# A third inner seven-product in a tuned Strassen-like MLP: product 2 of mixer 1 over a base in SBUF, with VectorE's sums reordered

## The chip, the cores and the metric

The kernel runs on one core of one Trainium2 chip. The metric is the device time of one execution in microseconds (us). Executions of one kernel mostly agree within 0.3%. Unless said otherwise, times are medians of several executions; the traces come from one profiled execution each.

In the profiles PE is TensorE (matmuls), PEld its weight loads, DVE is VectorE (here sums and additions), ACT is ScalarE (here copies and Gelu), POOL is GpSimd, and SP issues transfers (DMA). SBUF and PSUM are the two memories on the chip in which the kernel's tiles lie; its matmuls all write to PSUM. A "gap" below is the time by which a matmul starts later than the usual spacing of the matmuls before it would let it.

## The reference

The program is a pre-norm block: linear attention with a residual, then a token-mixing MLP with a residual. Only the first matmul of the MLP (here "mixer 1") matters for this change.

```python
def _B_ref(x, w1, b1, w2, b2):          # x: 1 x 2048 x 1024, w1: 2048 x 3584
    h = _layernorm(x, axis=-1)
    u = jnp.einsum("bsd,sf->bdf", h, w1) + b1      # mixer 1
    u = _gelu(u)
    y = jnp.einsum("bdf,fs->bds", u, w2) + b2      # mixer 2
    return (lambda x, *d: x.transpose(*d))(y, 0, 2, 1)
```

## The kernel before

Each block product is done with seven matmul products in place of eight (the Winograd form of Strassen). Two neighbouring block products ("sts") make one round. Products 1 and 5 of both are taken together and split once more into seven inner products of half the width: an `Inner` set. While TensorE works on a set, 16 matmuls of another product ("fill") are put between its seven steps, in four portions.

An `Inner` set keeps its results in two PSUM tiles: `ae` holds quarters a and e, `bc` holds quarters b and c. Keep `bc` in mind: b and c are two halves of one 512-column fp32 tile, which the kernel counts as one PSUM bank (its constant `BANK` is 512).

```python
psy = ...tile_pool(name="psy", bufs=NT, space=PSUM, ...)   # C;  NT = 2
psx = ...                                                  # B
psw = ...                                                  # A
psz = ...                                                  # inner sets (tags z0, z1): 8 such tiles in all

class Inner:
    ...
    def i1(self):
        ae = psz.tile([P, BANK], F32, tag="z0", bufs=1, name="psI0")
        bc = psz.tile([P, BANK], F32, tag="z1", bufs=1, name="psI1")
        self.a, self.e, self.b, self.c = ae[:, 0:HW], ae[:, HW:CW], bc[:, 0:HW], bc[:, HW:CW]
        self.mm(1, self.a, True)
        nc.scalar.copy(self.b, self.a)
    def i6(self):
        self.mm(6, self.b, False)
        nc.scalar.copy(self.c, self.b)
    def i2(self):
        self.mm(2, self.a, False)
        self.sink(0, 0, self.a)
    def i5(self):
        self.mm(5, self.e, True)
        self.es = cpool.tile([P, HW], F32, tag="es", name="es")
        nc.scalar.copy(self.es[:], self.e)            # ScalarE: "es"
    def i7(self):
        self.mm(7, self.c, False)
        self.sink_sum(1, 1, self.c, self.es[:])       # VectorE reads c
    def i3(self):
        self.mm(3, self.b, False)                     # TensorE writes b
        self.sink_sum(0, 1, self.b, self.es[:])
    def i4(self):
        self.mm(4, self.c, False)
        self.sink(1, 0, self.c)

    # Quad: the order of one set with its fill portions 0..3
    for f in (n.i1, after1, 0, n.i6, n.i2, 1, n.i5, n.i7, flush, 2, n.i3, 3, n.i4, flush): ...

    # Quad.run, one round of mixer 1 (cut)
    interleave(self.in1, [st.p4 for st in pend], start)   # set of product 1, fill: product 4 of the round before
    ...
    interleave(self.in5, [st.p6 for st in self.sts])      # set of product 5, fill: product 6
    ...                                                   # here VectorE sums for the next round (pre)
    for st in self.sts: st.p2()                           # 16 matmuls of 512 columns into A (PSUM)
    ...
    for st in self.sts: st.p7(...)
    for st in self.sts: st.p3()                           # the last evacuation is left to the next round
```

## Time and profile before

| | before |
|---|---|
| time, median of 3 | 571.77 us |
| span in the trace | 570.7 us |
| TensorE busy | 562.1 us (98%) |
| six rounds of mixer 1 with inner products | 143.0 us in this trace |
| a steady round | 23.57 us |

The head of the profile page (engine, busy time, share of the span, number of instructions), and the chain of waits by engine (the chain that ended last):

```profile
PE 562.1 (98%) x3049; PEld 289.9 (51%) x3064; DVE 388.2 (68%) x734; ACT 274.1 (48%) x573; POOL 1.8 (0%) x8
...
PE 87%; DVE 5%; DMA 4%; ACT 2%; issue 1%; SPq 0%; DVEq 0%
```

TensorE is the limit: it is nearly always busy, and 87% of the chain is its own work. VectorE and ScalarE matter only where TensorE waits for them.

The six rounds, each a stretch from its first inner matmul to the next round's. The columns are the stretch, its length, and the busy time of each engine with the number of instructions:

```profile
core 0: us, PE busy (x) PEld busy (x) DVE busy (x) ACT busy (x) POOL busy (x), PEclk, DMA share, GB/s
255.71:279.29 23.58, 23.58 (x137) 13.28 (x136) 14.78 (x32) 9.95 (x22) 0.00 (x0) 1.00 0.29 90
279.29:303.19 23.90, 23.80 (x137) 13.29 (x136) 12.17 (x26) 10.76 (x24) 0.00 (x0) 1.00 0.28 88
303.19:328.00 24.81, 23.80 (x138) 13.29 (x136) 14.10 (x28) 12.15 (x27) 0.00 (x0) 1.00 0.27 85
328.00:351.57 23.57, 23.57 (x138) 13.27 (x136) 12.80 (x26) 11.62 (x25) 0.00 (x0) 1.00 0.29 90
351.57:375.14 23.57, 23.57 (x137) 13.30 (x136) 12.81 (x26) 11.10 (x25) 0.00 (x0) 1.00 0.28 90
375.14:398.71 23.57, 23.57 (x137) 13.29 (x136) 7.59 (x15) 11.54 (x25) 0.00 (x0) 1.00 0.31 80
sum 143.00, PE 141.89 PEld 79.74 DVE 74.26 ACT 67.12 POOL 0.00; mean PE 23.65 PEld 13.29 DVE 12.38 ACT 11.19 POOL 0.00
```

Three rounds take 23.57 us. Rounds 2 and 3 take longer; there VectorE's timeline shows 1.58 and 2.49 us of idle that ended with the landing of weights, and evacuations queued behind it.

The waits of TensorE, window of mixer 1 (who waited for whom: us in total, times, longest):

```profile
PE psI L209 <- ACT psI L242: 1.0, 1, 1.0
PE psA L209 <- ACT psB L318: 0.4, 1, 0.4
```

One set of product 1 in a steady round, from the timeline (start, duration, engine, instruction; in brackets the idle time before it and what ended it). The matmuls at 331.69 are the set's seventh product, those at 332.88 its third:

```profile
331.69 0.60 PE L209 MATMUL psI<-hi,is 128*128 128x256 f16 x4
331.89 0.37 ACT L255 COPY es<-psI 128x256 f32<-128x256 f32 x1
...
332.12 0.81 PE L209 MATMUL psC<-hT,wq 128*128 128x512 f16 x3
332.39 0.43 DVE L209 TENSOR_TENSOR psA<-psI,es 128x256 f32<-128x256 f32 x1 [3.24 <-PE psI L209]
...
332.88 0.60 PE L209 MATMUL psI<-hE,is 128*128 128x256 f16 x4
```

The three fill matmuls start at 332.12. In this kernel 512-column matmuls start 0.216 us apart (16 take 3.455 us in the chain), so the third product (`psI<-hE,is`) could start at 332.77; it starts at 332.88. The profile prints no idle before it, because a 512-column matmul is drawn 0.379 us long, 0.163 us longer than its spacing.

### The profile page before, as it was taken

How to read it: one execution, taken by the hardware profiler on the slowest of the kernel's cores; microseconds unless marked ns; L12 is line 12 of the kernel's file. 1: busy time of each engine (PE TensorE's matmuls, PEld its weight loads, DVE VectorE, ACT ScalarE, POOL GpSimd, SP SyncE). 2: the span in 40 equal slices, each digit the busy share in tenths (PEclk: the TensorE clock that was granted, in tenths of full speed). 3: DMA queues.
4: the chain of work that ended last, by engine and by line, in shares of the span. 5: the costliest groups of instructions: out<-in, count | busy, mean ns of one | idle time of the engine just before them, and what ended most of it. 6: DMA issues, size and time to landing. Idle time of an engine off the chain costs nothing.

```text
span 570.7 us, 8133 instructions
## 1 busy us (share of the span) xinstructions
PE 562.1 (98%) x3049; PEld 289.9 (51%) x3064; DVE 388.2 (68%) x734; ACT 274.1 (48%) x573; POOL 1.8 (0%) x8
## 2 busy tenths in 40 slices
PE   8999999999999999999999999999999999999997
PEld 3444444454444444456555565554445655645643
DVE  6898888544776798965654735633989749658725
ACT  5747777667776777545445354453220311311211
POOL 1000000000000000000000000000000000000000
PEclk9999999999999999999999999999999999999999
DMA  9833432025673841104041340413892932912111
GB/s 302 288 74 76 92 74 38 19 94 180 189 231 102 276 168 74 56 0 149 1 148 40 108 148 1 148 57 75 211 250 92 241 92 75 284 48 75 38 46 47
DMA packets 86087, 67.13 MB, mean 118 GB/s; under 512 B 15762, under 2 KB 80032, under 8 KB 86048
## 3 DMA queue, kind: packets, MB, share of 16 engines
q1 hardware_dynamic: 85312, 65.94, 39.8%
q10 hardware_dynamic: 672, 0.66, 0.3%
q8 instruction: 24, 0.39, 0.3%
q14 instruction: 15, 0.12, 0.1%
q0 software_dynamic: 64, 0.01, 0.0%
HBM read 54.54 MB, written 8.91 MB: 111 GB/s over the span
## 4 chain that ended last, share of the span: by engine, by line
PE 87%; DVE 5%; DMA 4%; ACT 2%; issue 1%; SPq 0%; DVEq 0%
PE acc_t L209 16%; PE psC L209 14%; PE psB L209 12%; PE psI L209 11%; PE psA L209 6%; PE psB L797 4%; PE psC L797 4%; PE psA L797 4%; DMA wq<-in_B_w_dram 3%; PE acc_t L721 2%; PE psB L299 2%; PE psA L299 2%; PE acc_t L1066 2%; PE psE L797 2%; PE psC L299 2%; PE kvps L750 1%
## 5 line engine op out<-in xcount | busy, mean ns | idle before, releaser
L209 PEld LDWEIGHTS <-wq 128*128 128x128 bf16 (+1 forms) x653 | 63.4, 98 | 55.6 <-issue 1.0
L209 PEld LDWEIGHTS <-sa 128*128 128x128 f16 x651 | 63.7, 98 | 54.7
L209 PE MATMUL acc_t<-wo_sb,pqT 128*128 128x512 f16 x256 | 55.6, 379 | 0.0
L209 PEld LDWEIGHTS <-is 128*128 128x128 f16 x376 | 36.7, 98 | 19.4 <-issue 4.6
L209 PE MATMUL psC<-gs,wq 128*128 128x512 f16 (+2 forms) x210 | 45.0, 365 | 0.0
L209 PE MATMUL acc_t<-xnT,wq_sb 128*128 128x512 bf16 x188 | 43.1, 379 | 0.2
L209 PEld LDWEIGHTS <-pqT 128*128 128x128 bf16 x256 | 25.0, 98 | 30.5 <-issue 0.6
L171 DVE TENSOR_SCALAR e_sb<-e_sb 128x512 bf16<-128x512 bf16 x64 | 18.6, 290 | 27.9 <-ACT e_sb L167 27.3
L167 ACT ACTIVATE e_sb<-acc_t 128x512 bf16<-128x512 f32 x40 | 23.9, 597 | 24.5 <-PE acc_t L209 12.0
L797 PEld LDWEIGHTS <-xs 128*128 128x128 f16 x208 | 20.1, 98 | 23.3 <-DVE xs L783 1.3
L209 DVE TENSOR_TENSOR ot<-ot,hr 128x512 bf16<-128x512 bf16 (+2 forms) x27 | 11.2, 414 | 28.1 <-ACT ot L431 27.7
L209 DVE TENSOR_TENSOR e<-psI,es 128x256 f32<-128x256 f32 x20 | 8.5, 424 | 31.9 <-ACT es L255 19.3
L209 PEld LDWEIGHTS <-wq_sb 128*128 128x128 bf16 x192 | 18.5, 98 | 23.0 <-issue 1.3
L333 ACT COPY psC<-psB 128x512 f32<-128x512 f32 x22 | 12.5, 570 | 35.3 <-PE psB L209 30.5
L209 PE MATMUL psB<-hT,sa 128*128 128x512 f16 x112 | 28.7, 379 | 0.0
L209 DVE BATCH_NORM_STATS2 hst<-acc_t 128x6 f32<-128x512 f32 x32 | 21.3, 692 | 8.7 <-ACT h_bf L209 8.6
L797 PE MATMUL psA<-wkv,xnT 128*128 128x512 bf16 x98 | 26.4, 379 | 0.3
L209 DVE TENSOR_TENSOR psA<-psI,es 128x256 f32<-128x256 f32 x18 | 7.8, 433 | 26.9 <-PE psI L209 21.8
L209 PE MATMUL psA<-hO,wq 128*128 128x512 f16 x112 | 25.3, 379 | 0.4 <-ACT psB L318 0.4
L242 ACT COPY psI<-psI 128x256 f32<-128x256 f32 x19 | 6.9, 361 | 38.8 <-PE psI L209 38.8
L209 PE MATMUL psB<-hO,sa 128*128 128x512 f16 x112 | 25.3, 379 | 0.0
L209 PE MATMUL psC<-hT,sa 128*128 128x512 f16 x112 | 25.3, 379 | 0.0
(184 smaller groups left out, 1009.3 us busy)
## 6 DMA issues: line engine op xcount, KB each, us to landing
wq<-in_B_w_dram SPq DMA_DIRECT2D x14, 1024.0 KB, 7.9
wq<-in_B_w_dram SPq DMA_DIRECT2D x8, 1792.0 KB, 9.4
xr<-in_A_x_dram SPq DMA_DIRECT2D x16, 256.0 KB, 5.1
rdb<-rd_dram SPq DMA_DIRECT2D x32, 128.0 KB, 3.8
h_dram<-h_bf SPq DMA_DIRECT2D x16, 256.0 KB, 2.0
hr<-h_dram SPq DMA_DIRECT2D x32, 128.0 KB, 2.5
out_dram<-ot SPq DMA_DIRECT2D x31, 128.0 KB, 1.7
x_sb<-in_A_x_dram SPq DMA_DIRECT2D x15, 256.0 KB, 3.0
```

The source lines that it names most:

```text
L167: pin(nc.scalar.activation(e_sb[:], src, ACT.Exp))
L171: pin(nc.vector.tensor_scalar(e_sb[:], e_sb[:], 1.0, PHI_EPS, ALU.min, ALU.add))
L209: return (lambda *a, **kw: pin(op(*a, **kw))) if self.always or Held.on else op
L242: nc.scalar.copy(self.b, self.a)
L299: pe.matmul(ps[:, cols], lhsT=lhs[:, k, :], rhs=mv(k)[:, cols], start=(start and k == 0), stop=(k == self.nk - 1), skip_group_check=True,)
L333: nc.scalar.copy(self.C[:], self.B[:])
L721: mm = nc.tensor.matmul(pp[:, 0:CW], lhsT=xnT[:, kt, i * P:(i + 1) * P], rhs=wkv[:, kt, c * CW:(c + 1) * CW], start=(kt == 0), stop=(kt == ...
L750: pin(nc.tensor.matmul(kv_ps[b][:, sl, :], lhsT=pks[i % NPK][:, j * P:(j + 1) * P], rhs=vaugs[i % NVA][:, j, :], start=False, stop=(i == N ...
L797: pin(nc.tensor.matmul(ps[:], lhsT=lhs[:, k, :], rhs=rhs[:, k, :], start=(start and k == 0), stop=(k == hk2 - 1), skip_group_check=True,))
L1066: nc.tensor.matmul(qp[:, 0:SW], lhsT=wq_sb[:, kt, j * P:(j + 1) * P], rhs=xnT[:, kt, u * SW:(u + 1) * SW], start=(kt == 0), stop=(kt == ND ...
```

## The change

Product 2 becomes a third inner set (`Inner2`). Its base, the 512-column result A of product 1, no longer lies in PSUM but in SBUF (tiles a0 and a1), and VectorE adds the set's four results to it, in six additions of 256 columns. The fill of this set is product 7. That replaces 16 matmuls of 512 columns by 28 of 256 columns, that is, by 14 of 512. VectorE's sums for the next round move behind the evacuations (the steps that take finished results out of PSUM), and the evacuation of the round's last shared tile goes behind six of those sums. At the head, the last two combinations come after the last normalization.

```diff
+    class Inner2(Inner):
+        def i5(self):
+            self.mm(5, self.e, True)
+            for m in range(2):
+                self.sink(m, 1, self.e)
+        def i7(self):
+            self.mm(7, self.c, False)
+            self.sink(1, 1, self.c)
+        def i3(self):
+            self.mm(3, self.b, False)
+            self.sink(0, 1, self.b)
...
-        def begin(self):
-            self.A = psw.tile([P, BANK], F32, tag="w", name="psA1")
+        def begin(self, based=False):
+            if based:
+                self.A = pools["t"].tile([P, BANK], F32, tag=f"a{self.p % 2}", name="a1")
+            else:
+                self.A = psw.tile([P, BANK], F32, tag="w", name="psA1")
...
+        def sink2(self, m, h, ps):
+            t = self.sts[m].A[:, self.cols(h)]
+            dve.tensor_tensor(t, ps, t, ALU.add)
+
+        def run1(self, pend, nxt, on_p4):
+            def starting():
+                self.asums(5)
+                self.in5 = Inner(sts, 5, self.mov5, "i5", self.sink5, self.sum5)
+                self.in5.sums()
+                pend[1].p3_evac()
+                for st in sts:
+                    st.begin(based=True)
+            self.interleave(
+                self.in1, [st.p4 for st in pend], {"in": starting, "mid": partial(sts[0].asum, 6)}
+            )
+            sts[1].asum(6)
+            self.asums(7)
+            in2 = Inner2(sts, 2, self.mov2, "i1", self.sink2, None)
+            in2.sums()
...
+            self.interleave(self.in5, [st.p6 for st in sts])
...
+            self.interleave(in2, [st.p7_fill for st in sts], {
+                "third": lambda: sts[0].evac(0, 0, sts[0].A), "out": lambda: sts[1].evac(0, 0, sts[1].A),
+            })
+            if nxt is not None:
+                nxt.begin1()                      # sums of the next round's set of product 1
+            sts[0].p3()
+            sts[1].p3_mm()
... (the old run, with p2, and the order of the head are left out)
```

More of the change, by code (lines that the diff above doesn't have):

```diff
@@ L349, in p2, with p7_fill @@
                 self.evac(0, 0, self.A)
+        def p7_fill(self, ks=None, late=None):
+            self.mm(7, self.C, False, ks)
+            if self.whole(ks):
+                self.parts = [(0, CW, self.C)]
+                late.append(partial(self.evac_shared, 1, self.C))
         def p7(self, cut=None):
@@ L444, with __init__ @@
     class Quad:
-        def __init__(self, sts, mov1, mov5):
+        def __init__(self, sts, mov1=None, mov5=None, mov2=None):
             self.sts = sts
-            self.mov1, self.mov5 = mov1, mov5
-            self.after1 = nop
+            self.mov1, self.mov5, self.mov2 = mov1, mov5, mov2
         def cols(self, h):
@@ L467, in sum5, with interleave @@
             dve.tensor_tensor(self.sts[m].e[:, self.cols(h)], ps, es, ALU.add)
-        def pre(self, m):
-            if m == 5 and self.mov1 is not None:
-                self.in1 = Inner(self.sts, 1, self.mov1, "i1", self.sink1, self.sum1)
-                self.in1.sums()
-            for st in self.sts:
-                st.asum(m)
-            if m == 5:
-                self.in5 = Inner(self.sts, 5, self.mov5, "i5", self.sink5, self.sum5)
-                self.in5.sums()
-        def interleave(self, n, fs, after1=nop):
+        def interleave(self, n, fs, at={}):
             steps = [(f, k) for f in fs for k in range(self.sts[0].nk)]
@@ L495, in flush @@
                     late.pop(0)()
-            for f in (n.i1, after1, 0, n.i6, n.i2, 1, n.i5, n.i7, flush, 2, n.i3, 3, n.i4, flush):
-                fill(f) if isinstance(f, int) else f()
-        def asums_once(self, m):
-            for st in self.sts:
-                if m not in st.lhs:
-                    st.asum(m)
+            for f in (
+                n.i1, "in", 0, n.i6, n.i2, 1, n.i5, n.i7, flush, 2, "mid", n.i3, "third", 3, n.i4, "out", flush,
+            ):
+                if isinstance(f, int):
+                    fill(f)
+                else:
+                    (at.get(f, nop) if isinstance(f, str) else f)()
         def asums(self, m):
@@ L561, in run_first @@
             self.interleave(self.in5, [st.p6 for st in sts])
-            nxt.in1 = Inner(nxt.sts, 1, nxt.mov1, "i1", nxt.sink1, nxt.sum1)
-            nxt.in1.sums()
-            nxt.asums(5)
+            nxt.begin1()
             for st in sts:
@@ L568, in run_first @@
             sts[1].p3_mm()
-            def after1():
-                sts[1].p3_evac()
-                nxt.in5 = Inner(nxt.sts, 5, nxt.mov5, "i5", nxt.sink5, nxt.sum5)
-                nxt.in5.sums()
-                nxt.asums(6)
-            nxt.after1 = after1
-            return sts, nxt
-        def run(self, pend, nxt, on_p4=nop, before_p7=nop, on_p7=nop, cut=None):
-            interleave = self.interleave
-            if self.mov1 is not None:
-                def start():
-                    self.after1()
-                    for st in self.sts:
-                        st.begin()
-                interleave(self.in1, [st.p4 for st in pend], start)
-                self.asums_once(7)
-            else:
-                for st in self.sts:
-                    st.p1()
-                for st in pend:
-                    st.p4()
+            return sts, nxt
@@ new lines, in begin1 @@
+        def begin1(self):
+            self.in1 = Inner(self.sts, 1, self.mov1, "i1", self.sink1, self.sum1)
+            self.in1.sums()
+        def sink2(self, m, h, ps):
+            t = self.sts[m].A[:, self.cols(h)]
+            dve.tensor_tensor(t, ps, t, ALU.add)
+        def run1(self, pend, nxt, on_p4):
+            sts = self.sts
+            def starting():
[12 more added lines that the diff above has]
+            in2.sums()
@@ L594, in run @@
             on_p4()
             nxt = nxt()
-            for st in self.sts:
+            for st in sts:
                 st.shared_tile()
-            interleave(self.in5, [st.p6 for st in self.sts])
-            self.sts[0].finish()
-            self.asums_once(3)
-            pre = nxt.pre if nxt is not None else (lambda m: None)
-            pre(5)
-            for st in self.sts:
-                st.p2()
-            pre(6)
-            before_p7()
-            for st in self.sts:
-                st.p7(cut if st is self.sts[-1] else None)
@@ L609, in run @@
-            on_p7()
-            last = self.sts[-1]
-            for st in self.sts:
-                if st is last and nxt is not None:
-                    st.p3_mm()
-                    nxt.after1 = st.p3_evac
-                else:
-                    st.p3()
-            return self.sts, nxt
+            self.interleave(self.in5, [st.p6 for st in sts])
+            sts[0].finish()
+            self.asums(3)
+            self.interleave(in2, [st.p7_fill for st in sts], {
+                "third": lambda: sts[0].evac(0, 0, sts[0].A), "out": lambda: sts[1].evac(0, 0, sts[1].A),
+            })
@@ L619, in moving @@
+            if nxt is not None:
+                nxt.begin1()
+            sts[0].p3()
+            sts[1].p3_mm()
+            return sts, nxt
     def moving(E, O, T2, T3, T4):
@@ L1280, in h_scale, with normalize_h, combine_h @@
                 hs.activation(sc_all[:, i:i + 1], lnv[:], ACT.Exp, scale=-0.5)
-            def normalize_h(i):
+            def normalize_h(i, combined=True):
                 dst = hE if i % 2 == 0 else hO
                 hv.tensor_scalar(dst[:, i // 2, :], h_bfs.pop(i)[:], mv_all[:, i, 0:1], sc_all[:, i:i + 1], ALU.subtract, ALU.mult)
-                if i % 2 == 1:
-                    q = i // 2
-                    combine(hE[:, q, :], hO[:, q, :], hT2[:, q, :], hT3[:, q, :], hT4[:, q, :], hv)
+                if i % 2 == 1 and combined:
+                    combine_h(i // 2)
+            def combine_h(q):
+                combine(hE[:, q, :], hO[:, q, :], hT2[:, q, :], hT3[:, q, :], hT4[:, q, :], hv)
             for c in range(NDC):
@@ L1294, in first_sums @@
             def first_sums():
-                cur = Quad([Mixer1(0), Mixer1(1)], None, None)
+                cur = Quad([Mixer1(0), Mixer1(1)])
                 for m in (5, 6, 7, 3):
@@ L1348 @@
                     h_scale(i - 1)
-                    normalize_h(i - 2)
+                    normalize_h(i - 2, False)
                     normalize_h(i - 1)
@@ L1358 @@
             h_scale(NS - 1)
-            normalize_h(NS - 1)
+            normalize_h(NS - 1, False)
+            combine_h(NSP - 2)
+            combine_h(NSP - 1)
     accx.close()
@@ L1378 @@
     mov5, sums5 = inner_moving(hE[:, :, CW:D], NSP, inner1, "hi5")
+    mov2, sums2 = inner_moving(hO[:, :, 0:CW], NSP, inner1, "hi2")
     NQ1 = NFP // 2
@@ L1390, in quad1 @@
     def quad1(u):
-        return Quad([Mixer1(2 * u), Mixer1(2 * u + 1)], mov1, mov5)
+        return Quad([Mixer1(2 * u), Mixer1(2 * u + 1)], mov1, mov5, mov2)
     Held.on = True
@@ L1396 @@
     pend, nxt = cur.run_first(quad1(1), sums1)
+    sums2()
     for u in range(1, NQ1):
         cur = nxt
-        pend, nxt = cur.run(pend, lambda: quad1(u + 1) if u + 1 < NQ1 else None, on_p4=next_load1(u + 1))
+        pend, nxt = cur.run1(pend, lambda: quad1(u + 1) if u + 1 < NQ1 else None, next_load1(u + 1))
     Held.on = False
+    pend[1].p3_evac()
     for st in pend:
```

## The prediction

> **What bounds the kernel now.** TensorE: the page gives it 98% of the 570.7 us span, and the chain of waits gives it 87%. In mixer 1 the timeline repeats one round per pair of products; six rounds use the inner products (255.7 to 398.7 us). By windows they take 23.58, 23.90, 24.81, 23.57, 23.57, 23.57 us (sum 143.0), TensorE busy throughout except about 1 us in the third. VectorE is busy about 12.8 us of a round, ScalarE about 11.2. So only matmul time, and waits that the change adds or removes, count.
>
> **Removed and added per round.** Out: product 2, 16 matmuls of 512 columns, 3.455 us in the chain. In: seven inner products of four 256-column matmuls, 0.433 us each, 3.03 us; plus one more of the 0.1 us gaps that the timeline shows before the last-but-one inner product of every such set. Net -0.32 us: an undisturbed round should take 23.25 us. VectorE gains four inner sums (0.34 us each, start to start) and six 256-column additions (0.42 us): about 3.9 us a round, to roughly 16.7 of 23.5, not a limit by throughput. ScalarE gains two 0.36 us copies. Once, VectorE also pays 2.8 us for the moving sums of product 2.
>
> **Removed waits.** In rounds 2 and 3 VectorE sat waiting for weights (1.58 and 2.49 us of idle ended by the DMA), with evacuations queued behind; that reached TensorE as 0.23 and 0.97 us before an inner sixth product. The sums now come after the evacuations, about 4 us after the landing: about 1.5 us saved. At the head, putting the last two combinations after the last normalization should remove the 0.39 us wait of product 2 for the copy psB.
>
> **New wait.** The instruction order puts the Gelu of the previous round's last shared tile before the copy "es" of inner product 1 (before, it came two copies earlier, right after the first), because VectorE now evacuates that tile only after six sums. From the trace's start-to-start times I work out: es at 4.5 us into the round instead of 3.9; VectorE's next addition at 4.9, then a 0.61 us product-6 sum put between the two additions, the second at 5.9 instead of 5.5; ScalarE's queue then delivers the first copy of the inner set of product 5 at about 7.95 to 8.05 instead of 7.64. Its sixth product starts 0.41 us after that copy starts (seen in rounds 2 and 3), so at about 8.4 instead of 8.12: a stall of 0.2 to 0.4 us per round, eating most of the 0.32. Round 1, with the 2.8 us of moving sums in front, loses about 0.5. The Trainium skill ("TensorE: Matmul & The Clock Gate", Engine queue depths) says ScalarE and VectorE are strict FIFO; the trace agrees: evacuations start only after the stalled sums (rounds 2 and 3).
>
> **Sum.** Rounds: 6 x 23.25 + 0.5 + 5 x 0.28 = 141.4, against 143.0: -1.6. Head -0.4. Mixer 2 unchanged. Predicted 569.8 us, 8 in 10 between 567.8 and 571.4. Chances: faster by over 2% 0.01, within 2% 0.98, slower 0.01.
>
> **What would show it.** Right: rounds of about 23.5 us; idle TensorE of 0.2 to 0.4 us before the second inner product of the set of product 5, released by the ScalarE copy psI; no VectorE idle ended by the weight DMA; no gap in product 2 of the first round. If that idle is absent, rounds are 23.25 and the time is about 568.
>
> **What would make it wrong.** ScalarE slower reading the base from SBUF than from PSUM, lengthening every copy in that queue; the sums after the third set meeting the shared-tile evacuations later than I place them; the head or the start of mixer 2 (its first matmuls now stand inside the last round) stalling on VectorE.

## More of the kernel before

The Trainium skill ("Perfetto Trace Analysis", Tensor Engine Instruction) says that the end of a TensorE instruction is estimated, not observed. The trace agrees: the drawn end of the third fill matmul (332.12 + 0.81 = 332.93) lies after the start of the next one. A wait of up to 0.16 us can hide in that.

## The result, and the profile after

| | before | after |
|---|---|---|
| time, median (4 runs each) | 571.61 us | 574.27 us |
| six rounds in the trace | 143.0 us | 145.53 us |
| a steady round | 23.57 us | 24.20 us |
| VectorE busy in a steady round | 12.8 us | 16.4 us |

The ratio is 1.0045 (95% interval 1.0028 to 1.0063). A ratio is the mean time of one kernel's fast runs over that of the other's in the same rounds, so it is not quite the ratio of the medians. The change made the kernel slower by 2.7 us, or 0.45%; that is outside the noise. 569.8 us had been predicted, with a range up to 571.4.

The same parts of the page after:

```profile
PE 561.0 (98%) x3136; PEld 296.6 (52%) x3136; DVE 412.2 (72%) x798; ACT 278.5 (49%) x585; POOL 1.8 (0%) x8
...
PE 89%; DVE 5%; ACT 2%; DMA 1%; issue 1%; SPq 0%; DVEq 0%; ACTq 0%
```

The rounds of the changed kernel (rounds 2, 4 and 5 left out, they are 24.21, 24.21 and 24.20):

```profile
core 0: us, PE busy (x) PEld busy (x) DVE busy (x) ACT busy (x) POOL busy (x), PEclk, DMA share, GB/s
255.35:279.86 24.51, 23.41 (x149) 14.46 (x148) 18.36 (x40) 11.34 (x26) 0.00 (x0) 1.00 0.28 87
...
304.07:328.27 24.20, 23.40 (x149) 14.47 (x148) 16.40 (x37) 11.91 (x27) 0.00 (x0) 1.00 0.27 88
...
376.68:400.88 24.20, 23.72 (x151) 14.62 (x150) 14.95 (x33) 12.51 (x27) 0.00 (x0) 1.00 0.30 77
sum 145.53, PE 140.72 PEld 86.90 DVE 98.94 ACT 71.50 POOL 0.00; mean PE 23.45 PEld 14.48 DVE 16.49 ACT 11.92 POOL 0.00
```

The matmul work did shrink, yet every round is longer. TensorE's waits in mixer 1:

```profile
PE psI L209 <- DVE a L209: 4.8, 11, 0.8
PE psI L209 <- DVE e L209: 0.5, 1, 0.5
```

TensorE now waits for VectorE's additions, eleven times in the six rounds (the single wait for `e` comes before them). In which place? The set of product 1 in round 3:

```profile
307.43 0.72 ACT L407 ACTIVATE gE<-t,b_sb 128x512 f16<-128x512 f32 x1
307.76 0.60 PE L209 MATMUL psI<-hi,is 128*128 128x256 f16 x4
308.05 0.67 ACT L407 ACTIVATE gO<-psC,b_sb 128x512 f16<-128x512 f32 x1
...
308.19 0.81 PE L209 MATMUL psC<-hT,wq 128*128 128x512 f16 x3
308.62 0.36 ACT L255 COPY es<-psI 128x256 f32<-128x256 f32 x1
...
309.01 0.43 DVE L209 TENSOR_TENSOR a<-psI,es 128x256 f32<-128x256 f32 x1 [1.72 <-ACT es L255]
...
309.49 0.60 PE L209 MATMUL psI<-hE,is 128*128 128x256 f16 x4 [0.48 <-DVE a L209]
```

The fill starts at 308.19, so the third product (`psI<-hE,is`) could start at 308.84. It starts at 309.49, 0.65 us late, directly after VectorE's addition of the seventh product ended (309.01 + 0.43 = 309.44). That addition waits for the copy es, and es stands on ScalarE behind a Gelu of the last shared tile (`gE<-t`, 307.43). In the kernel before, that Gelu ran earlier in the set (at 329.19 in the round shown above, es at 331.89). The set of product 2, further on in that round:

```profile
321.52 0.60 PE L209 MATMUL psI<-hi,is 128*128 128x256 f16 x4
321.72 1.31 DVE L209 TENSOR_TENSOR a<-psI,a 128x256 f32<-128x256 f32 x3 [0.88 <-PE psI L209]
...
321.96 0.81 PE L209 MATMUL psC<-hT,sa 128*128 128x512 f16 x3
...
323.09 0.60 PE L209 MATMUL psI<-hO,is 128*128 128x256 f16 x4 [0.32 <-DVE a L209]
```

Here VectorE has two additions of the fifth product and then the one of the seventh in its queue (x3, 1.31 us), and the third product starts 0.48 us after the fill could have let it (321.96 + 0.65 = 322.61). In the set of product 5 the same gap is 0.10 us (315.35 + 0.65 = 316.00, start 316.10). So a steady round has 0.65 + 0.10 + 0.48 = 1.23 us of this one kind of wait, where the kernel before had two gaps of about 0.1. In round 1 the gap in the set of product 1 is 0.94 us (261.07 against 259.48 + 0.65), and there es is not late (done at 259.61): VectorE's addition starts only at 260.61, behind other work in VectorE's own queue.

What is odd: the third product writes b and needs nothing of c. VectorE's addition reads c.

### The profile page after: what moved, and what is told of

Read it like the earlier page. It is cut to its first block, busy times and chain, and to the rows that moved or that the text cites. A ratio compares the mean times of both kernels' runs of the same rounds, so it can differ in the third digit from the quotient of the medians.

```text
span 572.5 us, 8362 instructions
## 1 busy us (share of the span) xinstructions
PE 561.0 (98%) x3136; PEld 296.6 (52%) x3136; DVE 412.2 (72%) x798; ACT 278.5 (49%) x585; POOL 1.8 (0%) x8
## 4 chain that ended last, share of the span: by engine, by line
PE 89%; DVE 5%; ACT 2%; DMA 1%; issue 1%; SPq 0%; DVEq 0%; ACTq 0%
PE acc_t L209 18%; PE psI L209 15%; PE psB L209 14%; PE psC L209 13%; PE psB L801 4%; PE psC L801 4%; PE psA L801 4%; PE psA L209 3%; PE psB L313 2%; PE psA L313 2%; PE acc_t L1070 2%; PE psE L801 2%; PE psC L313 2%; PE acc_t L725 2%; DVE a L209 1%; DMA x_sb<-in_A_x_dram 1%
## 5 line engine op out<-in xcount | busy, mean ns | idle before, releaser
L209 PEld LDWEIGHTS <-wq 128*128 128x128 bf16 (+1 forms) x629 | 61.0, 98 | 46.8
L209 PEld LDWEIGHTS <-is 128*128 128x128 f16 x472 | 46.0, 98 | 29.5 <-issue 10.1
L209 DVE TENSOR_TENSOR a<-psI,a 128x256 f32<-128x256 f32 x36 | 14.7, 423 | 20.2 <-PE psI L209 18.9
L209 PE MATMUL psC<-hT,sa 128*128 128x512 f16 x112 | 28.3, 379 | 0.0
L242 ACT COPY psI<-psI 128x256 f32<-128x256 f32 x25 | 8.8, 354 | 37.9 <-PE psI L209 37.5
L246 ACT COPY psI<-psI 128x256 f32<-128x256 f32 x25 | 8.9, 357 | 33.0 <-PE psI L209 33.0
L801 PEld LDWEIGHTS <-xnT 128*128 128x128 bf16 x156 | 15.3, 98 | 18.5 <-issue 0.2
```

Source lines behind the costliest of these rows:

```text
L209: return (lambda *a, **kw: pin(op(*a, **kw))) if self.always or Held.on else op
L801: pin(nc.tensor.matmul(ps[:], lhsT=lhs[:, k, :], rhs=rhs[:, k, :], start=(start and k == 0), stop=(k == hk2 - 1), skip_group_check=True,))
```

## The experiments

Theory "bank": b and c lie in one PSUM bank, and the program therefore lets TensorE write b only when VectorE has finished with c. The Trainium skill ("PSUM — Partial Sum Buffer", PSUM bank collisions raise a hardware error) says that two engines must not access one bank in the same partitions at the same time, even at different columns, and that software has to keep them apart. The trace above agrees so far: b is written from 309.49, after the read of c ended at 309.44. Rivals: VectorE's added work is itself the cost ("VectorE load"); or ScalarE's late copy psI, as I had predicted ("ScalarE queue").

Every kernel gave correct results. A median of the kernel before, run on the same chip, goes with each call: 571.60 us for the first four, 571.49 us for the others, which ran on another chip.

### A bank of its own for c

```diff
         def i1(self):
             ...
+            if self.own:                       # mixer 1 only
+                self.c = psw.tile([P, BANK], F32, tag="w", name="psIc")[:, 0:HW]
             self.mm(1, self.a, True)
```

The base in SBUF has freed the bank pool of A, so there is room. All of VectorE's added work stays.

> The changed kernel with one edit: in mixer 1 the quarter c of every inner set lies in a PSUM bank of its own (the bank pool that the base left free), no longer beside b. Theory 'bank': the third product of each set (it writes b) waits until VectorE has read the result of the seventh (c), only because b and c share a bank. Then all these waits go: a steady round falls from 24.20 us to 22.9 to 23.1 us, and the time to about 566.5 us (565.5 to 568). Rival 'VectorE load' (the 24 us of added VectorE work is itself what costs) and rival 'ScalarE queue' (my prediction: the late copy psI before the sixth product of the product-5 set): the waits stay or move, 573.5 to 574.5 us.

Measured: 566.72 us (566.66 to 566.86), ratio to before 0.9906 (0.9885 to 0.9928). The set of product 1 in round 3, then that round and the sum of all six:

```profile
304.64 0.60 PE L209 MATMUL psIc<-hi,is 128*128 128x256 f16 x4
...
305.07 0.81 PE L209 MATMUL psC<-hT,wq 128*128 128x512 f16 x3
305.50 0.36 ACT L258 COPY es<-psI 128x256 f32<-128x256 f32 x1
...
305.72 0.60 PE L209 MATMUL psI<-hE,is 128*128 128x256 f16 x4
305.89 0.42 DVE L209 TENSOR_TENSOR a<-psIc,es 128x256 f32<-128x256 f32 x1 [1.72 <-ACT es L258]
...
308.48 0.39 ACT L245 COPY psI<-psI 128x256 f32<-128x256 f32 x1
...
308.78 0.38 ACT L481 COPY psB<-a 128x256 f32<-128x256 f32 x1
```

```profile
core 0: us, PE busy (x) PEld busy (x) DVE busy (x) ACT busy (x) POOL busy (x), PEclk, DMA share, GB/s
...
300.95:323.93 22.98, 22.98 (x149) 14.45 (x148) 16.22 (x37) 11.74 (x27) 0.00 (x0) 1.00 0.30 93
...
sum 138.14, PE 138.13 PEld 86.73 DVE 97.82 ACT 70.50 POOL 0.00; mean PE 23.02 PEld 14.46 DVE 16.30 ACT 11.75 POOL 0.00
```

The third product starts at 305.72, which is 305.07 + 0.65: at once. VectorE reads c (305.89 to 306.31) after TensorE has begun to write b (305.72); in two banks they overlap. VectorE's work in the round is still 16.22 us, and the copy es still stands behind the Gelu. The six rounds take 138.14 us in place of 145.53 (in place of 145.10 without the two matmuls of mixer 2 that stand in the changed kernel's last round and not in this one's). So the waits come from b and c sharing a bank (or a tile, see below), and "VectorE load" falls as the cost of a steady round.

Two reservations. First, the build changed more than the bank: in each of the six rounds the copy psI of the set of product 5 now runs ahead of a copy to psB (308.48, 308.78 above), and in the changed kernel it runs behind it. Part of the gain may belong to that; the ScalarE experiment below separates the two. Second, c has left not only its bank but also its tile. No run has b and c as two tiles in one bank, so whether the program keeps the accesses apart for a shared bank or for a shared tile stays open.

### The last shared tile evacuated ahead of the sums

```diff
             def starting():
+                pend[1].p3_evac()
                 self.asums(5)
                 ...
                 self.in5.sums()
-                pend[1].p3_evac()
```

> The changed kernel with one edit: the evacuation of the last shared tile of the round before stands ahead of the six sums on VectorE, so that its Gelu comes before, not after, the window in which the copy es is due. Theory 'bank': the copy es is in time, VectorE's addition of the seventh product too, and the gap before the third product of inner set 1 falls from 0.64 to 0.1 us in five rounds (in the first round VectorE does the same work before that addition, so nothing changes): steady round 23.66 us, time 571.3 to 571.9 us. Rival 'VectorE load': same work, same time, 574.3.

Measured: 571.81 us; steady round 23.66 us, as expected. Two timeline lines of the set of product 1 in round 3:

```profile
307.93 0.81 PE L209 MATMUL psC<-hT,wq 128*128 128x512 f16 x3
308.68 0.60 PE L209 MATMUL psI<-hE,is 128*128 128x256 f16 x4
```

From the fill at 307.93 to the third product it is 0.75 us now, 0.65 of it the three matmuls: a gap of 0.10 us. So in the steady rounds the late es is what sets the size of this wait. Round 1 stayed at 24.51 us, as expected; it got a 0.19 us idle of another kind there, the fifth product (e) waiting for ScalarE to read a. Those two also share a bank and a tile.

### The seventh product added first

```diff
         def i5(self):
             self.mm(5, self.e, True)
-            for m in range(2):
-                self.sink(m, 1, self.e)
+            self.sink(0, 1, self.e)
         def i7(self):
             self.mm(7, self.c, False)
             self.sink(1, 1, self.c)
+            self.sink(1, 1, self.e)
```

> The changed kernel with one edit: in the set of product 2, VectorE adds the seventh product before the second of the two additions of the fifth product. Theory 'bank': the gap before the third product of this set falls from 0.49 to about 0.1 us, in five rounds (in the last one two matmuls of mixer 2 fill it already): steady round 23.8 us, time 572.2 to 572.7 us. Rival 'VectorE load': same work, same time, 574.3.

Measured: 572.87 us, a little above the expected range; steady round 23.91 us in place of 23.8. The gap before the third product did fall to 0.10 us (fill at 321.39, third product at 322.14), but 0.1 us of the gain came back one step on: the fourth product (c) then followed the third by 1.39 us in place of 1.29, starting at 323.53 after VectorE's read of b (323.06 + 0.41 = 323.47). It is the same wait with b and c exchanged.

### The order of the sums alone, without the third set

In the changed kernel, product 2 is again 16 plain matmuls over A in PSUM; the new order of VectorE and the new head stay.

```diff
-            in2 = Inner2(sts, 2, self.mov2, "i1", self.sink2, None)
-            in2.sums()
 ...
-            self.interleave(in2, [st.p7_fill for st in sts], {...})
+            for st in sts: st.p2()
+            for st in sts: st.p7()
```

> One part of the change alone: the VectorE sums, the start of the round and the head as in the changed kernel, but product 2 as 16 plain matmuls over a base in PSUM, as before. Theory 'bank with a late es': the gap before the third product of inner set 1 is 0.5 to 0.7 us here too, a steady round takes 24.0 to 24.2 us, and the time is 573.5 to 574.5 us, slower than before by 2 to 3 us, though VectorE has no added work. Rival 'VectorE load' (the third inner set's additions and sums are the cost): no slower than before, 571 to 571.7 us.

Measured: 573.55 us, ratio 1.0026 (1.0005 to 1.0046); steady round 24.07 us, 0.50 longer than before. The wait is there with no third set at all:

```profile
308.83 0.60 PE L209 MATMUL psI<-hE,is 128*128 128x256 f16 x4 [0.44 <-DVE psA L209]
```

So, net of what it saves elsewhere, the reordering alone costs 1.95 us (573.55 against 571.60), most of the 2.7. "VectorE load" falls a second time, since this kernel has no added work there (12.7 us in a steady round).

### Both reorderings

The edits of the second and third experiments together, with the shared bank as it is.

> The changed kernel with both reorderings together (last shared tile evacuated ahead of the six sums; seventh product added before the second addition of the fifth), the shared bank left as it is. Theory 'bank': the two gains add up, steady round 23.3 us (22.94 of matmuls and three waits of 0.1), time 574.27 - 2.46 - 1.40 = 570.4 us (569.9 to 570.9). If the two waits hid one another, less than the sum: 571.3 to 571.8.

Measured: 571.00 us (570.13 to 571.55), slightly above the range expected; steady round 23.36 us in place of 23.3. In the rounds the two gains add up: 24.20 - 0.54 - 0.29 = 23.37. The time is about 0.6 us above what was expected. In the profiled execution (571.00 us) the rounds start at 256.25 us, against 255.35 in the changed kernel, so there the head ran later; the five runs span 1.4 us.

### Own bank and both reorderings

> Own bank for c together with both reorderings. Theory 'bank': with its own bank nothing waits in the steady rounds any more, so the reorderings have nothing left to give: 566.7 us (566.3 to 567.0), as with the own bank alone. If the waits of the changed kernel were a matter of VectorE's order rather than of the bank, this would be faster than the own bank alone by 0.5 us or more.

Measured: 566.82 us, the same as the own bank alone; steady round 22.98 us in both. Once the bank is not shared, these two reorderings have nothing left to give.

### The ScalarE copy that the prediction feared

The own-bank kernel, with one pair on ScalarE exchanged in each round, so that the copy psI of the set of product 5 stands where the changed kernel has it. The instruction lists of TensorE and VectorE are the same as with the own bank, and ScalarE's differs in these six pairs alone. That makes it the strictest test of the bank, too: in the traces ScalarE and VectorE run the same instructions in the same order as in the changed kernel, and the difference is that c has a bank of its own (besides that, two matmuls of mixer 2 stand after the last round and not in it).

```diff
+    (hs if self.own else nc.scalar).copy(self.b, self.a)      # keep its place in the queue
 ...
-    n.i3, "third", 3, n.i4, "out", flush,
+    n.i3, "third", 3, flush if n.own and n is getattr(self, "in1", None) else nop, n.i4, "out", flush,
```

> Own bank for c, and on ScalarE one pair swapped in each of the six rounds: the copy of inner set 5's first product (psI to psI) after, not before, the second copy of the sink of set 1's fourth product; nothing else differs. This is the order that the changed kernel has and on which my predicted stall rested. If that step of the prediction was right in itself, and only hidden in the changed kernel because TensorE came late anyway, the copy starts about 0.4 us later, at 7.95 us into the round instead of 7.53, and TensorE waits 0.3 to 0.4 us for it before the sixth product of set 5: steady round 23.3 us, time 568.3 to 569.0 us. If the step was wrong: no wait, 566.7 us.

Measured: 568.87 us; steady round 23.33 us, that is 0.35 more than 22.98. The set of product 1 in round 3, and the lines of the predicted wait:

```profile
305.75 0.81 PE L209 MATMUL psC<-hT,wq 128*128 128x512 f16 x3
...
306.39 0.60 PE L209 MATMUL psI<-hE,is 128*128 128x256 f16 x4
...
308.57 1.24 PE L209 MATMUL psB<-hT,sa 128*128 128x512 f16 x5
...
309.30 0.38 ACT L481 COPY psB<-a 128x256 f32<-128x256 f32 x1
...
309.61 0.34 ACT L209 COPY psI<-psI 128x256 f32<-128x256 f32 x1
...
310.00 0.60 PE L209 MATMUL psI<-hi,is 128*128 128x256 f16 x4 [0.19 <-ACT psI L209]
```

The third product starts at 306.39, 0.64 us after its fill began, which is at once: with the changed kernel's order on both engines, its wait of 0.65 us is gone. So moving c alone takes 574.27 us to 568.87; the other 2 us of the first experiment need its new order on ScalarE as well.

The copy starts at 309.61, 7.99 us into the round (which began at 301.62), and the sixth product 0.39 us after it, at 310.00. The fill before it starts at 308.57 and could have let it start at 309.65. The step that I had predicted is real. In the changed kernel it did not show, because TensorE came to this place 0.65 us late already and the copy was ready in time (it starts at 312.28 there, and the sixth product at 312.74, just when the fill lets it).

### The kernel before, a second trace

> The kernel before, for a second trace of it. The first trace came from an execution 0.9 us longer than the median. If the two waits of rounds 2 and 3 for late weights (0.33 and 1.24 us over 23.57) vary from one execution to the next, this trace has other values there, and the rest of the rounds is 23.57 us again; if they are part of the kernel, the same 1.57 us stand there again.

Measured: 571.13 us (one run, its state unknown). Its rounds 2 and 3 (the others are 23.57 or 23.58):

```profile
core 0: us, PE busy (x) PEld busy (x) DVE busy (x) ACT busy (x) POOL busy (x), PEclk, DMA share, GB/s
...
279.00:302.81 23.81, 23.77 (x137) 13.30 (x136) 12.82 (x27) 11.05 (x25) 0.00 (x0) 1.00 0.29 89
302.81:326.61 23.80, 23.76 (x137) 13.28 (x136) 13.35 (x27) 11.93 (x26) 0.00 (x0) 1.00 0.28 89
...
sum 141.90, PE 141.81 PEld 79.77 DVE 74.27 ACT 67.35 POOL 0.00; mean PE 23.64 PEld 13.29 DVE 12.38 ACT 11.22 POOL 0.00
```

The waits for late weights are there again but smaller: 0.24 and 0.23 us over 23.57, against 0.33 and 1.24 in the first trace. They stand in both traces, and their size varies. Against this trace, whose time is nearer to the median, the changed kernel's rounds lose 145.53 - 141.90 = 3.63 us.

## Why the prediction was wrong

It failed in one step, and one term was too large.

**The step that failed.** The prediction said: "plus one more of the 0.1 us gaps that the timeline shows before the last-but-one inner product of every such set". It took that gap as a fixed price. It is a wait for VectorE's addition of the seventh product, which was only just in time in the kernel before (0.11 us). The wait is as long as that addition is late. The prediction had worked out the lateness correctly (es at 4.5 us into the round; measured 308.62 - 304.07 = 4.55), and then followed it to the wrong place, further along ScalarE's queue. The chain from es to TensorE is much shorter: es, VectorE's addition, third product. In the set of product 1 that is 0.65 us against 0.1; in the set of product 2 it is 0.48 against 0.1. Together this adds 0.93 us per round: 23.25 + 0.93 = 24.18, measured 24.20. The cause under it is that b and c share a bank (or tile), which the prediction did not ask about: with c apart, and nothing else changed on the two helper engines, these waits are gone.

**Point by point.**

- TensorE as the limit, and the matmul arithmetic: right. With no waits at all a round takes 22.98 us; 23.57 less the two gaps (0.20) and less the saved work (0.42) is 22.95.
- VectorE "not a limit by throughput", about 16.7 us a round: right (16.4), and two experiments show that the amount of work costs nothing. Where an addition stands in VectorE's queue does cost: the 0.48 us in the set of product 2 are the wait for the seventh product's addition behind two added ones.
- The new wait at the sixth product of the set of product 5 (0.2 to 0.4 us): the mechanism was right, as the exchanged pair shows with 0.35 us. In the changed kernel it was absent, covered by the larger wait earlier in the round. So "if that idle is absent, rounds are 23.25" was wrong: it left out any other wait. The 1.9 us that the sum charges for this step (0.5 + 5 x 0.28) did not fall due, and so hid part of the miss: the waits before the third products cost 5.6 us over 6 x 23.25 instead (145.10 - 139.5).
- Round 1: "loses about 0.5" was too small. It takes 24.51 us, 1.26 over 23.25, with 0.94 us before the third product of the set of product 1.
- Weights: VectorE's idle before them is gone, as predicted. The term, "about 1.5 us saved", was mis-sized: it took one trace whose execution was 0.9 us above the median. The second trace shows 0.47 us.
- Head: the 0.39 us wait for psB is gone. In the trace a wait comes back a little later, before the third inner product of the round ahead of the six, where VectorE's addition is late in the same way: drawn as 0.48 us, by start times 0.64 against 0.10 before. The rounds start at 255.35 us, against 255.71 and 255.42 before.
- Mixer 2: the last round contains two of its matmuls (0.43 us), which fill the second wait there. No stall came of it.

Over the rounds: predicted 141.4 us, measured 145.53, or 145.10 without those two matmuls.

The version that beats both kernels is the change plus one edit, c in the bank that the change itself had freed: 566.72 us against 571.60 before.

## What to carry to other kernels

Before pricing a new order of work on the helper engines, list for every matmul what it waits for by PSUM bank and not only by operand: here a result read late held up the next write to the other half of its bank. Do not price a small gap that repeats at one place as a fixed cost (here it grew from 0.1 to 0.65 us) before you compare its end with the ends of other engines' work; go by start times, because the drawn ends of matmuls hid up to 0.16 us here. When a change frees a bank, try it on the pair of results that two engines touch in turn; here that was worth 7.5 us.

## What the Trainium skill lacked or had wrong

- "PSUM — Partial Sum Buffer" has the rule that two engines must not touch one bank at once, as an error to avoid. It lacks what obeying it costs in time: here 1.23 us in a round of 24.20, all of it gone with the two quarters in separate banks (round 23.33 with ScalarE's order held, where another wait of 0.35 us appears, and 22.98 without).
- "Perfetto Trace Analysis" (Optimization Strategy) says that the same gap repeating on the engine that should be saturated can mean too little SBUF or PSUM for the next tile. These gaps were no matter of allocation: the tile had been there since the first product of the set, and its other half was being read. (A further bank did cure them, as another home for c.)
- The same page says that matmul ends are estimated. It does not say that waits hide in this: in this trace a 512-column matmul is drawn 0.379 us long and spaced 0.216, so the 0.11 us wait of the kernel before is printed as no idle, and one of 0.65 as 0.48.
- The same page (Optimizing Scalar/DVE Operations) gives ScalarE about 93 ns of access overhead on SBUF and about 51 on PSUM. Copies of 256 columns into PSUM took 376 ns from the base in SBUF and 357 ns from PSUM here, a difference of 19 ns. The page does not say how its overhead divides between the memory that is read and the one that is written, so this shows what it lacks and not that it is wrong.
